# Idle tags for gelu rows, earlier block-sum stores, a later normalisation and slots by readiness in a two-layer attention and gMLP kernel

## The chip, the cores and the metric

The kernel runs on one core of one Trainium2 chip. A core has five engines with a queue of instructions each: TensorE (PE, matrix products), VectorE (DVE), ScalarE (ACT), GpSimd (POOL) and SyncE (SP, which here issues nearly all transfers). They run side by side and wait for one another through semaphores. The metric is the device time of one launch in microseconds (us), as the median of several runs; less is better. Beside the times there is one profiled execution, whose trace gives the start, the length and the releaser of every instruction.

## The reference: what is computed

One sequence of 2048 tokens with 512 features passes four blocks, each with a layer norm ahead of it and a residual: linear attention, gated MLP, linear attention, gated MLP, with the same weights in both layers. All is float32.

```python
# attention: 32 heads of 16
pq, pk = phi(q), phi(k)                    # phi(t) = (t + 1 if t > 0 else exp(t)) + 1e-6
kv  = einsum("bhsd,bhse->bhde", pk, v);  z = pk.sum over tokens
o   = (pq @ kv) / (pq . z + 1e-6);         x = x + o @ wo
# gated MLP: w_in is 512 x 1792, two halves of 896
z   = gelu(layernorm(x) @ w_in)
z1  = z[..., :896];  z2 = layernorm(z[..., 896:])
g   = w_sp @ z2 + b_sp[:, None]            # w_sp is 2048 x 2048, over the tokens
x   = x + (z1 * g) @ w_out
```

## The kernel before

**Arithmetic.** Each matrix operand is split into a high and a low part (`high`, L133, on ScalarE; `low`, L136, on VectorE), and each product is three matmuls: high by high, high by low, low by high (`mm3`, L147 to L149). TensorE is therefore fed by pairs of tiles, and a product starts when the high part is there.

**Order.** The order of the instructions of each engine is the order in which the program issues them; no scheduler moves anything. A token tile is 128 rows, so there are 16.

**Storage.** Fast memory is cut into slots: 23 `pages` of 128x512, six `quads` four times as large, four `bigs`, and eight banks of accumulators. `Slots.get` takes the free slot with the smallest count and `Slots.put` gives one back with a lag, so that a slot still being stored is not taken at once; it counts takings and not time. Beside them stand 16 tags (`ztag`), one for each token tile: tag i holds first the attention query of tile i, then (as `z_turn`) the normalised tile on its way through a transposition, block sums in between, and at last the z2 tile itself. `Views` (L63) cuts two spare quads into eight page-size views for the piece of work in P1 that follows; it hands them out in the order in which they came back, and turns to the pages only when no view is left.

**Stages of a layer.** P1 goes over the tiles: layer norm, projections of key and query, phi, and the accumulation of the key products. Beside that it prepares sums of blocks of w_sp, a row at a time, for later use (`Inner.staged`): load, add on VectorE, split, store to scratch as `n`; its slots come from `Views`. A short transition forms the weights of the attention output. P2 (`P2.run`, steps s = 1 to 18) works on four tiles at once, at different depths: `b_high`/`b_low` split the attention operand of tile s; `c` multiplies tile s - 1 and `c3` stores the new x, normalises it into `z_turn` and sends it through scratch memory (`yt`: a store and a load in another layout, then a 32x32 transpose on VectorE, L328); `d_high`/`d_low` split tile s - 2; `e` multiplies tile s - 3 by the second half of w_in, `e2` applies gelu, `e3` takes statistics, and `e4` normalises a tile that passed `e3`, for the last tile after the loop. In each step two rows of the first half of w_in are multiplied as well (`f`): the gelu row goes into a page (L924), is stored to scratch as `z1` (L927) and read by the gates much later. In layer one, step s ends with `sums.tick(s, TOKEN_TICKS)`: it stores the block sums of w_sp that were added one tick ago (`Sums.store`, L1194), loads the blocks for the next ones (L1187) into z tags that are free and else into pages, and adds them on GpSimd (`Sums.add`, L1201).

After P2 comes `tail` (L1017 on): the last f row (`last_f`), and products P3, P6, P7, P4 and P5 of a block scheme for the remaining f rows, with copies of results on ScalarE (`copied`, L997) and additions on VectorE (L1031). P4 is the spatial product by w_sp in a scheme with fewer products; each unit g of it needs a split weight (L1445 on ScalarE, L1454 on VectorE) and a split operand (L1424 to L1426, L1450, L1458), and TensorE runs 18 or 24 matmuls a unit (L1607 to L1609). In layer one `sums.tick(g, MIX_TICKS)` prepares the rest of the block sums beside it. Gates and the output product end the layer.

SyncE issues its transfers in program order. A transfer that has to wait for its data holds up all that are behind it.

Of the kernel before, what the change touches and what calls it, by code (L numbers as in the profile page):

```python
# [15 lines left out]
P = 128  # L16
# [3 lines left out]
NT = S // P  # L20
# [5 lines left out]
PHI_EPS = 1e-6  # L26
DEFER = 6
STORE, POOL = 6, 3
TOKEN_TICKS = {5: (5, 6), 6: (7,), 8: (8, 9), 9: (10,), 11: (11, 12), 12: (13,), 13: (14,), 14: (15,)}
MIX_TICKS = (1, 4, 7, 8, 10, 12, 14, 16, 20, 21, 23, 24, 26, 27, 29, 30, 32, 34, 35, 37, 38, 39, 40, 41)  # L30
MIX_UNITS = (11, 15, 18, 20, 25, 31, 36, 40), (1, 3, 5, 7, 9, 11, 13, 15)
MAKE_AT = 5, 8, 11
ROW_UNITS = range(1, 9)
# [4 lines left out]
class Slots:  # L38


    def __init__(self, pool, prefix, n):
        self.pool, self.prefix = pool, prefix
        self.free_list = [(0, i) for i in range(n)]
        self.held = {}
        self.count = 0

    def get(self, shape, dtype=F32):
        assert self.free_list, f"no {self.prefix} slot"
        first = min(self.free_list, key=lambda e: e[0])
        self.free_list.remove(first)  # L50
        n = first[1]
        self.count += 1
        t = self.pool.tile(shape, dtype, tag=f"{self.prefix}{n}", bufs=1, name=f"{self.prefix}{n}_{self.count}")
        self.held[id(t)] = (n, t)
        return t

    def put(self, *tiles, lag=0):
        for t in tiles:
            n, _ = self.held.pop(id(t))
            self.free_list.append((self.count + lag, n))  # L60


class Views:  # L63


    def __init__(self, pages, *tiles):
        self.pages = pages
        self.free_list = deque(t[:, n // 2, n % 2] for n in range(4) for t in tiles)
        self.held = {}

    def get(self, shape, dtype=F32):
        if not self.free_list:
            return self.pages.get(shape, dtype)
        t = self.free_list.popleft()
        self.held[id(t)] = t
        return t

    def put(self, t, lag=0):
        if id(t) not in self.held:
            self.pages.put(t, lag=lag)  # L80
            return
        self.free_list.append(self.held.pop(id(t)))

    def close(self):
        assert not self.held
# [3 lines left out]
def mixer_kernel(ctx: ExitStack, tc: tile.TileContext, x_in, wqkv, wo_d, win1_d, win2_d, wsp_d, bsp_d, wout_d,  # L89
                 ident_d, mask_d, out_d):  # L90
    nc = tc.nc
# [7 lines left out]
    pages = Slots(main, "pg", 23)  # L99
# [4 lines left out]
    PAGE = [P, 512]  # L104
    ztile = {}

    def ztag(i, shape, kind, dtype=F32):
        t = main.tile(shape, dtype, tag=f"z{i}", bufs=1, name=f"z{i}_{kind}")
        ztile[i] = t
        return t  # L110

    ident = consts.tile([P, P], F32, name="ident")
    ones_f = pages.get(PAGE)
    nc.vector.memset(ones_f, 1.0)

    mhalf = consts.tile([P, 1], F32, name="mhalf")
    nc.vector.memset(mhalf, -0.5)
# [17 lines left out]
    def low(l, src, h):  # L135
        nc.vector.tensor_sub(l, src, h.bitcast(F32))  # L136
# [155 lines left out]
    class Turn:  # L292
# [22 lines left out]
        def load(self, i):  # L315
            if i in self.d:
                self.raw[i] = load(self.d.pop(i).rearrange("(p m) f -> p (m f)", m=4))
# [15 lines left out]
    class P1:  # L333
# [158 lines left out]
        def start(self):  # L492

            nc.gpsimd.affine_select(ident, ones_f[:, 0:P], pattern=[[1, P]], compare_op=OP.is_equal, fill=0.0, base=0,
                                    channel_multiplier=-1)
            self.loadx(0)
            self.loadx(1)
            for w in (self.wk, self.wq):
                for _ in range(4):
                    w.fetch()  # L500
            self.loadx(2)
            self.loadx(3)
            m = pages.get(PAGE, F32R)
            nc.vector.tensor_copy(m, ones_f)
            b = banks.get(PAGE)

            def idle(n):
                for _ in range(n):
                    nc.tensor.matmul(b, m[:, 0:P], m, start=True, stop=True)

            idle(9)
            lows = deque()

            def wk_low():
                l, src, h, r = lows.popleft()
                low(l, src, h)
                pages.put(r)

            self.ln_a(0)
            self.ln_a(1)  # L520
            self.ln_b(0)
            self.wk.piece(lows=lows)
            wk_low()
            self.T_high(0)
            idle(2)
            banks.put(b)
            pages.put(m, ones_f)
            self.T_low(0)
            for _ in range(2):
                self.wk.piece(lows=lows)  # L530
                wk_low()
            self.ln_b(1)
            self.wk.piece(lows=lows)
            wk_low()
            b = self.kb[0] = banks.get(PAGE)
            h, l = self.xT[0]
            w = self.wk

            def mm(x, y, c, **kw):
                nc.tensor.matmul(b, x[:, c, :], y[:, c, :], start=kw.get("start", False), stop=kw.get("stop", False))  # L540

            mm(h, w.h, 0, start=True)
            mm(h, w.l, 0)
            mm(h, w.h, 1)
            mm(l, w.h, 0)
            mm(l, w.h, 1)
            mm(h, w.l, 1)
            mm(h, w.h, 2)
            mm(l, w.h, 2)
            self.T(1)  # L550
            mm(h, w.l, 2)
            mm(h, w.h, 3)
            mm(l, w.h, 3)
            mm(h, w.l, 3, stop=True)
            self.ln_a(2)
            for _ in range(4):
                self.wq.piece()
            self.ln_b(2)
# [210 lines left out]
    class P2:  # L769
# [139 lines left out]
                H1, H2 = self.p4.H1, self.p4.H2  # L909
                nc.vector.tensor_sub(z[:, H2], z[:, H1], z[:, H2])  # L910

        def f(self):
            if not self.fq:
                return False
            n, f = self.fq.popleft()
            h, l = self.xT[n]
            w = self.win1
            b = banks.get(PAGE)
            for c in range(4):
                mm3(b, (w.h[:, f, c, :], w.l[:, f, c, :]), (h[:, c, :], l[:, c, :]), c == 0, c == 3)  # L920
            if f == NF - 1 and n < 2:
                quads.put(*self.xT.pop(n))
            t = pages.get(PAGE)
            nc.scalar.activation(t, b, AF.Gelu_apprx_tanh)  # L924
            banks.put(b)
            z1s[self.L, n, f] = dram.tile(PAGE, F32, name=f"z1_{self.L}_{n}_{f}")
            nc.sync.dma_start(z1s[self.L, n, f], t)  # L927
            pages.put(t, lag=STORE)
            return True

        def gelu_out(self, n, f, t, src=None):
# [85 lines left out]
        def tail(self, p4):  # L1017
            self.last_f(3)
            U2, U3 = [], []
            for g in range(3):  # L1020
                y = banks.get(PAGE)
                self.product(y, "P3", g, start=True, stop=True)
                U2.append(self.copied(y))
                banks.put(y)
            quads.put(*self.xT.pop(3))
            self.fetch_sum(1)
            p4.fetch(0)
            p4.fetch(1)
            for g in range(3):
                self.product(self.X[g], "P6", g)  # L1030
                nc.vector.tensor_add(U2[g], U2[g], self.X[g])  # L1031
            quads.put(self.Tp[2])
            for g in range(3):
                self.product(self.X[g], "P7", g)
                U3.append(self.copied(self.X[g]))
            quads.put(self.Tp[3])
            p4.prepare(0, 0)
            p4.fetch(2)
            for g in range(3):
                self.product(self.X[g], "P4", g, stop=True)  # L1040
                self.gelu_out(2, g + 3, pages.get(PAGE), self.X[g])
                banks.put(self.X[g])
            quads.put(self.Tp[4])
            self.win1.free()
            p4.prepare(1, 1)
            p4.fetch(3)
            for g in range(3):
                y = banks.get(PAGE)
                self.product(y, "P5", g, start=True, stop=True)
                for n, f, t in ((3, g + 3, U3[g]), (3, g, U2[g])):  # L1050
                    nc.vector.tensor_add(t, t, y)
                    p4.outs.append((n, f, t))
                banks.put(y)
            quads.put(self.Tp[1])
            p4.prepare(None, 2)
# [20 lines left out]
        def run(self, sums):  # L1076
# [3 lines left out]
            for s in range(1, NT + 3):  # L1080
# [58 lines left out]
                if s > 6:  # L1139
                    self.e4(s - 4)  # L1140
                self.xturn.load(s - 1)
                if s >= 3:
                    self.e(s - 3)
                    self.e2(s - 3)
                if s >= 6:
                    self.e3(s - 3)
                self.f()
                self.f()
                self.side(s)
                if self.L == 0:  # L1150
                    make.step(s)
# [7 lines left out]
                w1.fetch()  # L1159
                if self.L == 0:  # L1160
                    sums.tick(s, TOKEN_TICKS)
            self.e4(NT - 1)
            self.win2.free()


# [185 lines left out]
    class P4:  # L1351
# [395 lines left out]
        def run(self, nxt):  # L1747
# [13 lines left out]
            for g in range(n):  # L1761
# [8 lines left out]
                if self.nest_late:  # L1770
                    self.sums.tick(g, MIX_TICKS)
                    if g == 34:
# [88 lines left out]
    sums = Sums()  # L1861
# [45 lines left out]
```

## Time and profile before

| | us |
|---|---|
| median of 3 runs | 1373.98 |
| lowest and highest | 1371.97, 1375.28 |
| profiled execution | 1371.57 |
| its span, first to last instruction | 1369.8 |
| TensorE busy | 1358.0 |
| VectorE busy | 1024.6 |
| ScalarE busy | 636.7 |
| GpSimd busy | 467.5 |

Times in the rows below count from the start of the span. A row of the timeline gives the start, the length, the engine, the line, the operation and, in square brackets, how long the engine stood idle before it and what released it (`<-`). The first column of a slice table is the stretch, then follow its length, the busy time of each engine, the granted clock of TensorE, the share of the transfer engines in use and the rate in GB/s. Tiles are named by their slots: pg a page, qd a quad, bg a big one, z_q, z_z, z_sum and z_turn the uses of a tag. Where a transfer row has `x2`, two issues stand together. In layer one the residual additions of P2 (L843) stand from 146.7 to 311.7 us, and the first matmul of the spatial product (L1608) starts at 354.2.

### The profile page before, as it was taken

What the parts mean: (1) busy time and instruction counts of PE and PEld (TensorE: products, weight loads), DVE (VectorE), ACT (ScalarE), POOL (GpSimd) and SP (SyncE); (2) the same over time, 40 slices, a digit from 0 to 9 for tenths busy, and PEclk for the clock granted to TensorE, in tenths of its full rate; (3) what the DMA queues carried; (4) which work ended last, traced back from release to release, by engine and by line L of the source; (5) the groups of instructions that cost most, each with busy time, mean ns of one, the idle gap of its engine ahead of it and who ended that gap; (6) DMA issues with size and microseconds to landing.
All of it is one profiled execution on the core that took longest, in us unless ns stands there. A gap on an engine that the chain in (4) does not pass through costs nothing.

```text
span 1369.8 us, 18327 instructions
## 1 busy us (share of the span) xinstructions
PE 1358.0 (99%) x6087; PEld 1132.0 (83%) x6087; DVE 1024.6 (75%) x1581; ACT 636.7 (46%) x1021; POOL 467.5 (34%) x551
## 2 busy tenths in 40 slices
PE   9999999999999999999999999999999999999998
PEld 7788888878888888888888888888888888888887
DVE  7886888767855888986678768887767798978642
ACT  6675544435442443442456655444455534533310
POOL 2334385453143337426421133633230011412340
PEclk9999999999999999999999999999999999999999
DMA  5673378886788988895776533666568798569652
GB/s 187 203 233 95 123 251 266 281 270 196 241 284 284 304 273 276 274 391 180 221 253 202 194 101 114 210 205 206 189 197 277 226 336 322 187 200 314 216 186 89
DMA packets 184496, 310.18 MB, mean 226 GB/s; under 512 B 15696, under 2 KB 67920, under 8 KB 180304
## 3 DMA queue, kind: packets, MB, share of 16 engines
q1 hardware_dynamic: 172736, 262.73, 58.6%
q0 software_dynamic: 8064, 39.85, 8.3%
q10 hardware_dynamic: 3600, 6.42, 1.3%
q8 instruction: 48, 0.79, 0.2%
q14 instruction: 48, 0.39, 0.1%
HBM read 211.68 MB, written 97.26 MB: 226 GB/s over the span
## 4 chain that ended last, share of the span: by engine, by line
PE 71%; DVE 3%; DMA 2%; issue 1%; ACT 1%; POOL 0%; SPq 0%; DVEq 0%; ACTq 0%; POOLq 0%
PE bank L149 11%; PE bank L147 10%; PE bank L148 10%; PE bank L1608 9%; PE bank L1607 9%; PE bank L1609 9%; PE bank L1540 4%; PE bank L1541 4%; PE bank L1538 4%; PE bank L989 1%; PE bank L991 1%; PE bank L990 1%; DMA yt<-z_turn 1%; DMA pg<-yt 0%; DVE st L262 0%
## 5 line engine op out<-in xcount | busy, mean ns | idle before, releaser
L1608 PE MATMUL bank<-qd,pg 128*128 128x512 f32 x544 | 211.7, 389 | 0.5 <-DVE qd L1454 0.5
L1609 PE MATMUL bank<-qd,pg 128*128 128x512 f32 x544 | 211.6, 389 | 0.0
L1607 PE MATMUL bank<-qd,pg 128*128 128x512 f32 x544 | 211.6, 389 | 0.0
L1454 DVE TENSOR_TENSOR qd<-qd,qd 128x1024 fp32r<-128x1024 f32 x104 | 142.3, 1368 | 65.5 <-ACT qd L1445 65.0
L1445 ACT ACTIVATE qd<-qd 128x1024 fp32r<-128x1024 f32 x104 | 110.0, 1058 | 121.9 <-DVE qd L1454 44.1
L149 PE MATMUL bank<-qd,pg 128*128 128x512 f32 x380 | 149.0, 392 | 0.5 <-DVE pg L136 0.4
L133 ACT ACTIVATE pg<-pg 128x512 fp32r<-128x512 f32 (+1 forms) x146 | 89.2, 620 | 123.1 <-DVE pg L328 38.2
L266 POOL TENSOR_SCALAR rs<-mv 128x1 f32<-128x1 f32 x95 | 42.6, 448 | 273.4 <-DVE mv L264 269.3
L1629 POOL TENSOR_TENSOR bg<-bg,pg 128x512 f32<-128x512 f32 x56 | 91.7, 1648 | 107.0 <-DMA pg<-z 98.1
L136 DVE TENSOR_TENSOR pg<-pg,pg 128x512 fp32r<-128x512 f32 (+1 forms) x143 | 108.4, 759 | 20.4 <-ACT pg L133 15.8
L1608 PEld LDWEIGHTS bank<-qd,pg 128*128 128x128 f32 x544 | 102.1, 188 | 22.1 <-DVE qd L1454 0.9
L1607 PEld LDWEIGHTS bank<-qd,pg 128*128 128x128 f32 x544 | 102.1, 188 | 21.2
L1609 PEld LDWEIGHTS bank<-qd,pg 128*128 128x128 f32 x544 | 102.1, 188 | 21.2
L1201 POOL TENSOR_TENSOR pg<-pg,pg 128x512 f32<-128x512 f32 x45 | 67.3, 1495 | 137.6 <-DMA pg<-in_wsp_dram 116.8
L147 PE MATMUL bank<-qd,pg 128*128 128x512 f32 x284 | 110.9, 391 | 0.5 <-ACT pg L133 0.5
L148 PE MATMUL bank<-qd,pg 128*128 128x512 f32 x284 | 110.6, 390 | 0.0
L147 PE MATMUL bank<-bg,qd 128*128 128x448 f32 x256 | 95.1, 371 | 2.8 <-ACT qd L133 2.7
L149 PE MATMUL bank<-bg,qd 128*128 128x448 f32 x256 | 94.5, 369 | 0.2
L148 PE MATMUL bank<-bg,qd 128*128 128x448 f32 x256 | 94.2, 368 | 0.0
L328 DVE STREAM_TRANSPOSE pg<-pg 128x512 f32<-128x512 f32 x79 | 86.0, 1088 | 6.0 <-DMA pg<-yt 2.9
L1540 PE MATMUL bank<-qd,pg 128*128 128x512 f32 x224 | 87.4, 390 | 0.3 <-DVE qd L1454 0.3
L1538 PE MATMUL bank<-qd,pg 128*128 128x512 f32 x224 | 87.2, 389 | 0.0
(218 smaller groups left out, 3193.3 us busy)
## 6 DMA issues: line engine op xcount, KB each, us to landing
qd<-s SPq DMA_DIRECT2D x64, 512.0 KB, 4.0
qd<-n POOLq DMA_DIRECT2D x32, 1024.0 KB, 7.5
pg<-in_wsp_dram SPq DMA_DIRECT2D x84, 256.0 KB, 4.7
qd<-in_wsp_dram SPq DMA_DIRECT2D x40, 512.0 KB, 4.2
pg<-z SPq DMA_DIRECT2D x56, 256.0 KB, 3.9
n<-pg SPq DMA_DIRECT2D x54, 256.0 KB, 4.5
s<-pg SPq DMA_DIRECT2D x53, 256.0 KB, 4.4
x<-pg SPq DMA_DIRECT2D x48, 256.0 KB, 2.7
```

The costliest lines, as they stand in the source:

```text
L136: nc.vector.tensor_sub(l, src, h.bitcast(F32))
L147: nc.tensor.matmul(out, ah, bh, start=start, stop=False)
L148: nc.tensor.matmul(out, ah, bl, start=False, stop=False)
L149: nc.tensor.matmul(out, al, bh, start=False, stop=stop)
L1445: nc.scalar.activation(wh, r, AF.Copy)
L1454: nc.vector.tensor_sub(wl, r, wh.bitcast(F32))
L1538: m(out[i], h[:, o, f], w[:, o, 0], start=first and name in ("P1", "P2", "P5"), stop=False, skip_group_check=True)
L1540: m(out[i], h[:, o, f], w[:, o, 1], start=False, stop=False, skip_group_check=True)
L1607: m(out, h[:, o], w[:, 0, j, :], start=start, stop=False, skip_group_check=True)
L1608: m(out, h[:, o], w[:, 1, j, :], start=False, stop=False, skip_group_check=True)
L1609: m(out, l[:, o], w[:, 0, j, :], start=False, stop=stop, skip_group_check=True)
L1629: nc.gpsimd.tensor_tensor(u, u, z1, op=OP.mult)
```

## The change

Six edits, all in the order or the place of work that is done before and after alike.

1. `Views` keeps with each view the count at which it is due back. `get` hands out a view only if it is due, or if no page is due either; else it takes a page.
2. `f` takes an optional tag. In both layers the first gelu row of step s goes into tag s + 2 where that is below 16, and in layer one the second goes into the tag that `SPARE_TAGS` names for the step; else a page is used as before.
3. `TOKEN_TICKS` gives each fetch of block sums one tag, the number of its step, where before some got two and the fetches at 6, 9, 12, 13 and 14 a tag one higher. The other two blocks go to pages.
4. In layer one `sums.store()` is called in the middle of each step of P2, right behind the load of the turned tile, and no longer at its end.
5. `e4` of the last tile moves from the end of the P2 loop into `tail`, behind the three P3 products and their copies.
6. The first entry of `MIX_TICKS` is 2 instead of 1. And `ones_f`, a page of ones for the start, is set in two instructions, the first 128 columns and then the rest.

```diff
-TOKEN_TICKS = {5: (5, 6), 6: (7,), 8: (8, 9), 9: (10,), 11: (11, 12), 12: (13,), 13: (14,), 14: (15,)}
-MIX_TICKS = (1, 4, 7, 8, ...
+TOKEN_TICKS = {at: (at,) for at in (5, 6, 8, 9, 11, 12, 13, 14)}
+SPARE_TAGS = {6: 7, 8: 7, 9: 10, 11: 10, 14: 15, 16: 15}
+MIX_TICKS = (2, 4, 7, 8, ...
...
 class Views:
-        self.free_list = deque(t[:, n // 2, n % 2] for n in range(4) for t in tiles)
+        self.free_list = deque((0, t[:, n // 2, n % 2]) for n in range(4) for t in tiles)
...
     def get(self, shape, dtype=F32):
-        if not self.free_list:
+        now = self.pages.count
+        if not self.free_list or (self.free_list[0][0] > now and any(r <= now for r, _ in self.pages.free_list)):
             return self.pages.get(shape, dtype)
-        t = self.free_list.popleft()
+        _, t = self.free_list.popleft()
...
     def put(self, t, lag=0):
...
-        self.free_list.append(self.held.pop(id(t)))
+        self.free_list.append((self.pages.count + lag, self.held.pop(id(t))))
...
-    nc.vector.memset(ones_f, 1.0)
+    nc.vector.memset(ones_f[:, 0:P], 1.0)
...
+            nc.vector.memset(ones_f[:, P:], 1.0)
             nc.vector.tensor_copy(m, ones_f)
...
-        def f(self):
+        def f(self, tag=None):
...
-            t = pages.get(PAGE)
+            t = pages.get(PAGE) if tag is None or tag >= NT else ztag(tag, PAGE, "out")
...
             nc.sync.dma_start(z1s[self.L, n, f], t)
-            pages.put(t, lag=STORE)
+            if id(t) in pages.held:
+                pages.put(t, lag=STORE)
...
         def tail(self, p4):
...
                 banks.put(y)
+            self.e4(NT - 1)
             quads.put(*self.xT.pop(3))
...
         def run(self, sums):
...
                 self.xturn.load(s - 1)
+                if self.L == 0:
+                    sums.store()
                 if s >= 3:
                     self.e(s - 3)
...
-                self.f()
-                self.f()
+                self.f(s + 2)
+                self.f(SPARE_TAGS.get(s) if self.L == 0 else None)
...
-            self.e4(NT - 1)
             self.win2.free()
```

More of the change, by code (lines that the diff above doesn't have):

```diff
@@ L28 @@
 STORE, POOL = 6, 3
-TOKEN_TICKS = {5: (5, 6), 6: (7,), 8: (8, 9), 9: (10,), 11: (11, 12), 12: (13,), 13: (14,), 14: (15,)}
-MIX_TICKS = (1, 4, 7, 8, 10, 12, 14, 16, 20, 21, 23, 24, 26, 27, 29, 30, 32, 34, 35, 37, 38, 39, 40, 41)
+TOKEN_TICKS = {at: (at,) for at in (5, 6, 8, 9, 11, 12, 13, 14)}
+SPARE_TAGS = {6: 7, 8: 7, 9: 10, 11: 10, 14: 15, 16: 15}
+MIX_TICKS = (2, 4, 7, 8, 10, 12, 14, 16, 20, 21, 23, 24, 26, 27, 29, 30, 32, 34, 35, 37, 38, 39, 40, 41)
 MIX_UNITS = (11, 15, 18, 20, 25, 31, 36, 40), (1, 3, 5, 7, 9, 11, 13, 15)
```

## The prediction

> **What bounds the kernel now.** I read the page first, then the waits of TensorE, then the instructions around each wait in the timeline, engine by engine.
>
> ```profile
> span 1369.8 us, 18327 instructions
> PE 1358.0 (99%) x6087; PEld 1132.0 (83%) x6087; DVE 1024.6 (75%) x1581; ACT 636.7 (46%) x1021; POOL 467.5 (34%) x551
> ```
>
> TensorE is busy for 1358.0 of 1369.8 us. The change removes no matmul, so it can only win back idle time, 11.8 us in all, and what the clock loses around it. The waits of TensorE (total, times, longest):
>
> ```profile
> PE bank L147 <- ACT qd L133: 2.7, 2, 2.0
> PE bank L989 <- DVE pg L1031: 1.0, 1, 1.0
> ```
>
> The timeline of TensorE at four of its waits, all in layer one, and the slice table for the longest:
>
> ```profile
> 63.75 0.39 PE L149 MATMUL bank<-pg,pg 128*128 128x512 f32 x1
> 64.67 0.50 PE L147 MATMUL bank<-qd,pg 128*128 128x512 f32 x1 [0.53 <-ACT pg L133]
> ...
> 65.74 0.39 PE L147 MATMUL bank<-qd,pg 128*128 128x512 f32 x1
> ...
> 284.70 0.47 PE L147 MATMUL bank<-bg,qd 128*128 128x448 f32 x1 [2.01 <-ACT qd L133]
> ...
> 340.03 0.39 PE L990 MATMUL bank<-qd,pg 128*128 128x512 f32 x1
> 340.26 0.39 PE L991 MATMUL bank<-qd,pg 128*128 128x512 f32 x1
> 341.64 0.50 PE L989 MATMUL bank<-qd,pg 128*128 128x512 f32 x1 [0.99 <-DVE pg L1031]
> ...
> 364.90 0.39 PE L1607 MATMUL bank<-qd,pg 128*128 128x512 f32 x1
> 365.80 0.50 PE L1608 MATMUL bank<-qd,pg 128*128 128x512 f32 x1 [0.51 <-DVE qd L1454]
> ...
> 371.41 0.39 PE L1608 MATMUL bank<-qd,pg 128*128 128x512 f32 x1
> ```
>
> ```profile
> 280.00:300.00 20.00, 17.81 (x74) 15.04 (x75) 13.28 (x22) 9.19 (x15) 9.04 (x14) 0.91 0.91 302
> ```
>
> Undisturbed matmuls of 512 columns start 0.23 us apart (340.03 to 340.26). A wait costs its start-to-start time less 0.23. From 63.75 to 65.74 four intervals took 1.99 instead of 0.92: 1.07 lost. From 340.26 to 341.64: 1.38 less 0.23 is 1.15. From 364.90 to 365.80: 0.90 less 0.23 is 0.67. The wait before 284.70 cost 2.01, and the clock granted in its slice is 0.91 of full speed, some 0.09 x 20 = 1.8 more: 3.8 together.
>
> **Part by part.** *Spare quads by readiness (Views).* The timelines of ScalarE and VectorE ahead of 64.67:
>
> ```profile
> 60.28 0.63 ACT L133 ACTIVATE qd<-qd 128x512 fp32r<-128x512 f32 x1 [2.09 <-DMA n<-qd]
> ...
> 63.99 0.63 ACT L133 ACTIVATE pg<-pg 128x512 fp32r<-128x512 f32 x1 [0.69 <-PE bank L148]
> ```
>
> ```profile
> 62.10 0.69 DVE L417 SCALAR_TENSOR_TENSOR z_q<-bank,z_q 128x512 f32<-128x512 f32 x1 [2.22 <-ACT z_q L416]
> 62.81 1.09 DVE L328 STREAM_TRANSPOSE pg<-pg 128x512 f32<-128x512 f32 x1
> ```
>
> At 60.28 the block-sum piece writes a view of a spare quad whose last store (DMA n<-qd) has not landed; ScalarE stands for 2.09. The query projection's exponentials are queued behind it, VectorE's L417 waits 2.22 for them, the transpose L328 follows at 62.81, and the operand that TensorE wants is written at 63.99 to 64.62, 0.05 before 64.67. The named releaser of 63.99 (a matmul) is long done; the transpose is what came last. The change gives this piece a page that is already free, so the chain moves up by about 2 us, more than the 1.07 that TensorE lost. Gain between 0 (if what follows catches up) and 1.07; I take 1.0, because nothing in that row set but ScalarE's wait was late.
>
> *Gelu rows in idle tags, sums stored mid-step.* What VectorE waits for in layer one's second half, and SyncE's issues there:
>
> ```profile
> 264.59 0.88 DVE L136 TENSOR_TENSOR pg<-pg,pg 128x512 fp32r<-128x512 f32 x1 [1.81 <-DMA z<-pg]
> ...
> 279.38 0.69 DVE L136 TENSOR_TENSOR pg<-pg,pg 128x512 fp32r<-128x512 f32 x1 [1.59 <-DMA z<-pg]
> ```
>
> ```profile
> 276.05 0.86 SPq L927 DMA_DIRECT2D z<-pg  x2
> ...
> 278.20 1.62 SPq L1194 DMA_DIRECT2D s<-z_sum  x2
> ```
>
> Both L136 write the low half of the attention operand (b_low) into a page whose gelu row is still being stored. With gelu rows in z tags the first wait goes. The second stays: the slots are reused in count order, and in the new order the page that b_low of step 13 draws is that of a block sum, whose store now is issued in the very place of the gelu row's, right behind the yt load (276.05 instead of 278.20). So it lands when the gelu row landed, and L136 starts at about 279.4 again. No DMA is added or dropped; the three sum stores move ahead of two gelu-row stores and two win_sums stores, each of which goes to scratch that nobody reads for many steps. What decides the wait at 284.70 is further on:
>
> ```profile
> 284.69 0.57 SPq L313 DMA_DIRECT2D yt<-z_turn  x1
> 290.18 0.32 SPq L129 DMA_DIRECT2D pg<-yt  x1
> ```
>
> The chain of waits runs through the turn of each tile: store to scratch (yt), landing 5.5 us later, load, transpose, split, the matmuls of e. SyncE issues in order and its count per step is unchanged. So I put this part at 0 on the path, between -3.8 (the wait at 284.70 goes with its clock loss) and the worst price of the next paragraph.
>
> *One tag per fetch, tags in use sooner.* A tag now carries a sum, its store, and the next turned tile closer together: ScalarE's z_turn (L277) waits for the sum's store to land. The landing times of all sum stores between 250 and 330 us (least, median, most), the z_turn of step 15, and SyncE's place right behind the yt load, which the sum stores take:
>
> ```profile
> DMA to landing us min/median/max: 3.3/3.7/4.2
> ```
>
> ```profile
> 306.89 0.80 ACT L277 ACTIVATE z_turn<-pg,nb,rs 128x512 f32<-128x512 f32 x1
> ```
>
> ```profile
> 302.07 0.94 SPq L228 DMA_DIRECT2D win_sums<-pg  x2
> ```
>
> The z_sum goes second, at about 302.55, and with 3.7 lands at 306.25, 0.6 ahead of the z_turn. Steps 14 and 16 are built alike. I take 0; with the longest landing, 4.2, and no margin in one of them, 0.5 at worst. Behind z_turn stand the yt store and, one step on, e.
>
> *Last tile normalised in the tail (e4).* POOL, ScalarE and VectorE before 341.64:
>
> ```profile
> 337.40 1.32 POOL L271 TENSOR_SCALAR nb<-mv,rs 128x1 f32<-128x1 f32 x1
> ```
>
> ```profile
> 338.76 1.14 ACT L277 ACTIVATE z_z<-z_z,nb,rs 128x896 f32<-128x896 f32 x1 [2.17 <-POOL nb L271]
> 339.80 0.58 ACT L924 ACTIVATE pg<-bank 128x512 f32<-128x512 f32 x1
> ```
>
> ```profile
> 340.89 1.29 DVE L1031 TENSOR_TENSOR pg<-pg,bank 128x512 f32<-128x512 f32 x2 [1.62 <-ACT pg L997]
> ```
>
> The normalisation of tile 15 holds ScalarE for 2.17 us until POOL's nb; the gelu row of last_f (L924), the U2 copies (L997), and VectorE's L1031, for which TensorE waits, are queued behind it. Moved behind the three P3 products, it lets L924 start 338.76 - 2.17 = 336.6, over 3 us sooner, and the copies with it. VectorE had been idle for 1.62 before 340.89, so L1031 can start at 339.3 and end its first half (1.29 / 2) near 339.9, ahead of 340.49, where TensorE would want it. All 1.15 is gained, at least 0.99 less the 0.23 of a matmul if the copies come late. It also lets SyncE's gelu-row store go sooner, and so the first two spatial fetches behind it. Cost: the normalisation of tile 15 itself ends some 1 to 2 us later; the spatial product reads that tile only in its later operands. I count 0 for it, and the copies cover it.
>
> *First block sum of the spatial product one unit later (MIX_TICKS).* POOL's three additions, and VectorE beside and after them:
>
> ```profile
> 359.44 4.55 POOL L1201 TENSOR_TENSOR pg<-pg,pg 128x512 f32<-128x512 f32 x3 [19.07 <-PE bank L1608]
> ```
>
> ```profile
> 361.20 1.64 DVE L1424 TENSOR_TENSOR z_z<-z_z,z_z 128x384 f32<-128x384 f32 x1
> 362.87 1.53 DVE L1425 TENSOR_TENSOR pg<-z_z,z_z 128x384 f32<-128x384 f32 x1
> ...
> 364.53 1.21 DVE L1454 TENSOR_TENSOR qd<-qd,qd 128x1024 fp32r<-128x1024 f32 x1
> ...
> 366.26 0.55 DVE L1424 TENSOR_TENSOR z_z<-z_z,z_z 128x384 f32<-128x384 f32 x1
> ...
> 367.52 1.22 DVE L1454 TENSOR_TENSOR qd<-qd,qd 128x1024 fp32r<-128x1024 f32 x1
> ```
>
> Two subtractions of 128x384 took 1.64 and 1.53 beside the additions, and 0.55 without: 2.07 in excess, which made L1454 end at 365.74, 0.06 before 365.80. Without it L1454 ends near 363.7, with over 1 us to spare, and the 0.67 is gained. One unit later the same 2.07 falls on the operand whose split ended at 368.74 with that excess still in it and that TensorE wants from 371.41: 2.67 to spare, 2.0 after the gain. Gain 0.67, at worst 0.67 less 2.07.
> [...]
>
> *The memset in two pieces.*
>
> ```profile
> 0.97 0.48 DVE L114 MEMSET pg<- 128x512 f32 x1 [0.97 <-PEq L1896]
> ```
>
> The same 512 columns are set, in one more instruction; 0, at most 0.48 either way. Layer two gets the tags and the readiness rule as well; its waits are none of the ones above, and I count 0.
>
> The sum: 1.0 + 1.15 + 0.67 = 2.8 us, rounded up to 2.9 for the slower first matmul behind each wait (0.50 against 0.39 at 341.64 and 365.80). The profiled execution took 1371.57 us (its span is 1369.8), 2.4 below the median of the runs, 1373.98. So the profiled execution would become 1368.7 and the median about **1371.1**.
>
> **The rivals.** *One: the wait at 284.70 goes too.* If the sum's store lands sooner than the gelu row's did, or TensorE's wait is cut enough that the clock holds, up to 3.8 more is won, 1367.3. For it: one of the two store waits is gone. Against: the other is replaced, the yt chain ends last, and the row of the waits has a second wait of 0.7 (2.7 less 2.0) on the same chain that would absorb part of it; I would expect about half, 1369.
> [...]
>
> *Two: half of it does not show.* The 1.0 at 64.67 is given back, because what follows in that stage is paced by loads and not by TensorE; 1.9 is left, 1372.1, no measurable change. If the page drawn at step 13 is freed later than reckoned (its store kept at 278.20, landing at 281.9, 2.6 after 279.38), the loss of 2.6 eats almost all: 1373.7.
>
> *Three: slower, by tags.* Under the load of this stage other stores of the same size take longer to land (x rows, the same stretch, least, median, most):
>
> ```profile
> DMA to landing us min/median/max: 3.8/5.2/6.6
> ```
>
> If the sum stores, now among them, take 6.6 instead of 3.7, the z_turn of step 15 starts 2.3 late (6.6 less the 4.3 between 302.55 and 306.89), and with it yt, transpose and e; if steps 14 and 16 do the same, three of them add up to 6.9, less 2.9: +4.0, 1378.0. It decides from a landing of 4.3 us on; at 5.2 it is three times 0.9, and 1373.8.
>
> **How the numbers follow.** A change of 0.2%, 2.7 us, is about what a measurement of this kernel can tell from none; from 1373.98 that is 1371.2 to 1376.7. The forecast has 0.50; its own range, 1369.8 to 1372.3, has a little more than half below 1371.2, so 0.28 faster and 0.22 same. Rival one has 0.16, all faster; two 0.14, all same; three 0.20, of which 0.03 for its mild form (5.2), same, and 0.17 slower. Faster 0.44, same 0.39, slower 0.17. The range, 1366.8 to 1377.0, takes in all of one and two and the lower half of three; it leaves out some 0.1 above and what the scatter of the runs adds.
>
> **What would show it.** In the changed profile: no wait of ScalarE on n<-qd near 60 and none of TensorE at 64.7; no wait on L1031 near 338 and on L1454 near 362; the long additions of POOL one unit later. The wait of e near 282 should still be there with a granted clock near 0.9. Wrong it would be if that wait is gone, or if ScalarE's z_turn waits on a sum store.

## The result and the profile after

| | before | after |
|---|---|---|
| median, 12 runs each (us) | 1373.88 | 1369.03 |
| lowest and highest | 1371.61, 1376.39 | 1367.73, 1371.06 |
| profiled execution | 1371.57 | 1370.24 |

The ratio is 0.9965 with a 95% interval of 0.9956 to 0.9974, so 4.9 us were won (3.6 to 6.0), where 2.9 were forecast. The two profiled executions differ by 1.3 only: that of before lies 2.3 below its median, that of after 1.2 above its own. One pair of profiles shows where the time goes, but not how much of it goes there in the usual execution; the experiments have to tell that.

The page of the changed kernel, its first lines, and the waits of TensorE (total, times, longest; the changed kernel's L149 is L147 of before, L135 is L133, L512 is L509):

```profile
span 1368.5 us, 18313 instructions
...
PE 1356.4 (99%) x6087; PEld 1131.3 (83%) x6087; DVE 1026.7 (75%) x1582; ACT 637.6 (47%) x1021; POOL 468.0 (34%) x551
```

```profile
PE bank L149 <- ACT qd L135: 5.2, 4, 1.5
PE bank L512 <- DVE pg L507: 2.0, 1, 2.0
PE bank L151 <- DVE pg L138: 0.5, 2, 0.3
```

The waits on L1031 (tail) and L1454 (spatial product) are gone, and so is that at 64.7. In their place stands a longer sum for one line: the product e waits four times for its split operand (5.2 us, where the line had 2.7 in two waits). The slice table of the changed kernel (stretch, length, busy time of TensorE, its weight loads, VectorE, ScalarE and GpSimd, clock, transfers' share, GB/s):

```profile
60.00:80.00 20.00, 20.00 (x90) 16.54 (x89) 18.21 (x31) 16.44 (x29) 6.79 (x11) 1.00 0.82 259
...
280.00:300.00 20.00, 17.08 (x77) 13.79 (x76) 11.46 (x19) 9.08 (x15) 9.93 (x16) 1.00 0.87 278
300.00:320.00 20.00, 17.52 (x78) 13.74 (x77) 15.41 (x28) 8.42 (x13) 7.05 (x12) 1.00 0.67 229
...
340.00:360.00 20.00, 20.00 (x90) 16.57 (x89) 13.31 (x24) 8.23 (x13) 0.70 (x2) 1.00 0.63 207
360.00:380.00 20.00, 20.00 (x90) 16.57 (x89) 18.75 (x26) 12.10 (x18) 5.88 (x4) 1.00 0.78 263
```

TensorE is full in the three slices (60 to 80, 340 to 360, 360 to 380) where the prediction found a wait that goes, and short by 2.9 and 2.5 us in the two slices of layer one's second half. The timeline of TensorE there:

```profile
283.17 0.47 PE L149 MATMUL bank<-bg,qd 128*128 128x448 f32 x1 [1.32 <-ACT qd L135]
294.32 0.47 PE L149 MATMUL bank<-bg,qd 128*128 128x448 f32 x1 [1.50 <-ACT qd L135]
306.39 0.47 PE L149 MATMUL bank<-bg,qd 128*128 128x448 f32 x1 [0.89 <-ACT qd L135]
316.04 0.47 PE L149 MATMUL bank<-bg,qd 128*128 128x448 f32 x1 [1.48 <-ACT qd L135]
```

Before, the four were 2.01 (with a drop of the clock), none worth naming, 0.66 and 0.12. Two of the waits behind them are ones that the prediction named: on VectorE (b_low of step 13), as a wait that stays, and on ScalarE (z_turn of step 16), at 0.5 at worst:

```profile
277.84 0.69 DVE L138 TENSOR_TENSOR pg<-pg,pg 128x512 fp32r<-128x512 f32 x1 [1.79 <-DMA s<-pg]
```

```profile
316.34 0.81 ACT L279 ACTIVATE z_turn<-pg,nb,rs 128x512 f32<-128x512 f32 x1 [0.35 <-DMA s<-z_sum]
```

The gelu row's store (1.59, z<-pg) has been replaced by the sum's (1.79, s<-pg) as the releaser of b_low. The trip of the turned tile through scratch, on SyncE's queue, is longer than before:

```profile
283.12 1.03 SPq L315 DMA_DIRECT2D yt<-z_turn  x1
289.40 0.32 SPq L131 DMA_DIRECT2D pg<-yt  x1
...
295.43 0.61 SPq L315 DMA_DIRECT2D yt<-z_turn  x1
301.72 0.32 SPq L131 DMA_DIRECT2D pg<-yt  x1
```

Each load waits 6.3 us for the store ahead of it to land; in the profile of before the two took 5.5 and 5.4. In the second profiles (below) it is 5.9 and 5.6 for the changed kernel, 4.9 and 5.0 for the kernel before.

### The profile page after: what moved, and what is told of

It is laid out like the page before. It is cut to its first block, busy times and chain, and to the rows that moved or that the text cites. A ratio compares the mean times of both kernels' runs of the same rounds, so it can differ in the third digit from the quotient of the medians.

```text
span 1368.5 us, 18313 instructions
## 1 busy us (share of the span) xinstructions
PE 1356.4 (99%) x6087; PEld 1131.3 (83%) x6087; DVE 1026.7 (75%) x1582; ACT 637.6 (47%) x1021; POOL 468.0 (34%) x551
## 3 DMA queue, kind: packets, MB, share of 16 engines
q1 hardware_dynamic: 172736, 262.73, 58.9%
## 4 chain that ended last, share of the span: by engine, by line
PE 76%; DVE 3%; DMA 3%; ACT 1%; issue 1%; POOL 1%; SPq 0%; DVEq 0%; ACTq 0%; POOLq 0%
PE bank L151 11%; PE bank L149 11%; PE bank L150 11%; PE bank L1613 9%; PE bank L1614 9%; PE bank L1615 9%; PE bank L1546 4%; PE bank L1544 4%; PE bank L1547 4%; DMA yt<-z_turn 1%; PE bank L994 1%; PE bank L993 1%; PE bank L995 1%; DMA pg<-yt 1%; DVE pg L138 1%
## 5 line engine op out<-in xcount | busy, mean ns | idle before, releaser
L1460 DVE TENSOR_TENSOR qd<-qd,qd 128x1024 fp32r<-128x1024 f32 x104 | 143.4, 1380 | 67.8 <-ACT qd L1451 67.4
L135 ACT ACTIVATE pg<-pg 128x512 fp32r<-128x512 f32 (+1 forms) x146 | 89.3, 620 | 123.8 <-DVE pg L330 47.2
L268 POOL TENSOR_SCALAR rs<-mv 128x1 f32<-128x1 f32 x95 | 42.2, 444 | 266.6 <-DVE mv L266 258.0
L1207 POOL TENSOR_TENSOR pg<-pg,pg 128x512 f32<-128x512 f32 x48 | 70.8, 1475 | 138.0 <-DMA pg<-in_wsp_dram 113.9
L149 PE MATMUL bank<-qd,pg 128*128 128x512 f32 x284 | 110.9, 390 | 0.2 <-ACT pg L135 0.2
L149 PE MATMUL bank<-bg,qd 128*128 128x448 f32 x256 | 94.6, 370 | 5.2 <-ACT qd L135 5.2
```

The source lines that it names most:

```text
L149: nc.tensor.matmul(out, ah, bh, start=start, stop=False)
L1460: nc.vector.tensor_sub(wl, r, wh.bitcast(F32))
```

## The experiments

Each was compared with the kernel before on its own chip; "won" is the ratio's distance from 1, times 1374.

| run | what | median (us) | ratio, interval | won (us) |
|---|---|---|---|---|
| e1_rest | all but tags and stores | 1369.24 | 0.9957, 0.9944 to 0.9971 | 5.9 |
| e2_p2 | tags and stores alone | 1375.07 | 0.9995, 0.9986 to 1.0004 | 0.7 |
| e5_views | readiness alone | 1371.09 | 0.9970, 0.9958 to 0.9981 | 4.1 |
| e6_tail | normalisation in the tail alone | 1373.51 | 0.9993, 0.9984 to 1.0001 | 1.0 |
| e7_mix | first block sum later, alone | 1374.30 | 0.9995, 0.9986 to 1.0004 | 0.7 |
| e8_early_fetch | the changed kernel, sums' transfers ahead of the yt load | 1367.40 | 0.9948, 0.9936 to 0.9961 | 7.1 |
| e9_mid_tick | and GpSimd's additions with them | 1364.48 | 0.9922, 0.9909 to 0.9935 | 10.7 |
| e10_mid_tick_x | and the x store behind the yt store | 1366.29 | 0.9934, 0.9922 to 0.9946 | 9.1 |

**The two halves of the change, and second profiles.** My theory on record was: three waits go, 2.9 us, and the second half of layer one stays as it is (A). Against it stood that the second half is worth as much again (B), and that arriving there earlier changes what its transfers meet (C).

e1_rest:

```diff
 # e1_rest, against after.py (f itself as before, too)
-TOKEN_TICKS = {at: (at,) for at in (5, 6, 8, 9, 11, 12, 13, 14)}
-SPARE_TAGS = {6: 7, 8: 7, 9: 10, 11: 10, 14: 15, 16: 15}
+TOKEN_TICKS = {5: (5, 6), 6: (7,), 8: (8, 9), 9: (10,), 11: (11, 12), 12: (13,), 13: (14,), 14: (15,)}
...
-                if self.L == 0:
-                    sums.store()
...
-                self.f(s + 2)
-                self.f(SPARE_TAGS.get(s) if self.L == 0 else None)
+                self.f()
+                self.f()
```

> Before plus the readiness of the spare quads, the last tile's normalisation in the tail, the first block sum one unit later and the memset in two; nothing of the gelu rows, tags and sum stores. Theory A (on record: these three waits go, the attention and gMLP half of layer one stays as it is): 2.9 us faster than before, ratio 0.9979, and in the profile no wait of TensorE at 64.7, 341.6 and 365.8, the wait of 2 us near 284 as before. Theory B (the stores and tags are worth as much again in the median run, and the profile of before was a good one): the same 2.9 here. Theory C (the earlier arrival at the second half is what helps, because it changes what its transfers meet): 4 to 5 us faster here, ratio near 0.9967.

e2_p2 is the kernel before with just these edits of the change and none of the others.

> Before plus the gelu rows and block sums in tags and the sum stores mid-step; nothing else of the change. Theory A: within 0.5 us of before, ratio 1.000; in the profile VectorE waits for a sum's store instead of a gelu row's at b_low of step 13. Theory B: 2 us faster, ratio 0.9985. Theory C: no change, or slightly slower, up to 1 us, as the four waits of the profile of the changed kernel (1.32, 1.50, 0.89, 1.48) against those of before (2.01 with its clock loss, 0.66, 0.12) would have it.

> The kernel before, unchanged, for a second profile of it. If the waits of TensorE between 280 and 320 us vary from execution to execution (theory B), they come to more here than the 2.8 us of idle and 1.9 us of lost clock in the first profile, by 1 to 3 us, and the time is nearer to 1374; if they do not (theory A), they are the same within 0.5 us.

> The changed kernel, unchanged, for a second profile. Its first had 5.2 us of waits for the split operand of the second half (1.32, 1.50, 0.89, 1.48) and 1370.24 us, 1.2 over its median. Theory B: those waits come to 1 us or more less here, with a time near 1369. Theory A: the same within 0.5 us.

e1_rest won 5.9 us and its median, 1369.24, is that of the whole change; e2_p2 won 0.7 with an interval that holds 1. So the second half's edits are not worth the 2 us that B gave them, and A is right about the second half and wrong about the size of the rest. C's number came, but not where C looked for it: the profile of e1_rest has the same waits in the second half as that of before, 1.98, 0.67 and 0.35 against 2.01, 0.66 and 0.12. So C falls too. In the profile of e2_p2 b_low of step 13 waits for a sum's store, as A expected, but for 3.16 us, and the waits of e there sum to 4.6.

The second profiles (1372.81 before, 1368.56 after) are split. B expected of the changed kernel 1 us or more less of these waits, and they sum to 3.9 instead of 5.2; it expected of the kernel before 1 to 3 us more than the first profile lost there, and the waits sum to 3.5 with the clock at 1.00, less than the 2.8 us and the lost clock of the first. So the second half does vary from execution to execution. The hint came from another stage: in the second profile of before TensorE also loses time at 56, 96 to 99 and 118, in the stage of the spare quads, where the first had none.

**The three other edits one by one.**

```diff
 # e5_views, before.py with
-        if not self.free_list:
+        now = self.pages.count
+        if not self.free_list or (self.free_list[0][0] > now and any(r <= now for r, _ in self.pages.free_list)):
             return self.pages.get(shape, dtype)
...
 # e6_tail, before.py with
+            self.e4(NT - 1)
             quads.put(*self.xT.pop(3))
...
-            self.e4(NT - 1)
             self.win2.free()
...
 # e7_mix, before.py with
-MIX_TICKS = (1, 4, 7, 8, ...
+MIX_TICKS = (2, 4, 7, 8, ...
```

> Before plus the readiness of the spare quads alone. Step of the prediction: 1.0 us faster, the one wait at 64.7. Rival: the late ScalarE of that stage costs TensorE more in a usual execution than in the first profile of before; the second profile of it lost 2.6 us between 30 and 120 us of the span (at 56, 64, 96, 99 and 118) and the kernel with the second half's edits alone 4.0, against 0.7 with readiness. Then 2 to 3 us faster, ratio 0.9978 to 0.9985, and 0.7 us or so lost there in its profile.

> Before plus the last tile's normalisation in the tail alone. Step of the prediction: 1.15 us faster, ratio 0.9992, no wait of TensorE for VectorE's L1031 in the tail. Rival: the earlier first fetches of the spatial product are worth something too: up to 2 us, ratio 0.9985.

> Before plus the first block sum of the spatial product one unit later, alone. Step of the prediction: 0.7 to 0.8 us faster, ratio 0.9995, no wait for L1454 near 366; the additions lengthen VectorE's operations one unit later without a wait of TensorE. [...] The three alone should add up to what the kernel with all three won, 4 to 6 us, if they do not act on one another; if the sum stays below 3.5, they do.

They won 4.1, 1.0 and 0.7 us: 5.8 in sum, and 5.9 together, so nothing shows that they act on one another, though each figure is uncertain by about 1 us. The tail and the block sum came out near the predicted 1.15 and 0.67, but the interval of each reaches to 1; the profiles, which settle these two, follow below. Readiness was sized too small: 1.0 against 4.1, with an interval from 2.6 to 5.8. The memset in two pieces was tried only together with the others; in the first 20 us TensorE is neither ahead nor behind with it, beyond the 0.5 us by which the profiles without it differ among themselves.

Where its time comes from is seen in the profile of e6_tail, which still has the old `Views`. The slice of that stage, first of e6_tail and then of e5_views:

```profile
30.00:125.00 95.00, 92.95 (x398) 73.31 (x397) 75.24 (x120) 65.61 (x111) 32.38 (x46) 1.00 0.67 197
```

```profile
30.00:125.00 95.00, 94.96 (x418) 78.00 (x417) 77.16 (x123) 67.44 (x114) 33.21 (x47) 1.00 0.67 203
```

In the same 95 us TensorE starts 20 matmuls fewer in e6_tail, some 4.5 us of work at 0.23 each. Without readiness the five profiles had 415 (the first one of before), 410, 408, 402 and 398 there, with it all seven had 417 to 419. The prediction worked from the best of the five. In e6_tail the waits of TensorE, of ScalarE between 60 and 120 us, and VectorE's transpose at the end of the stage read:

```profile
PE bank L147 <- ACT pg L133: 1.1, 1, 1.1
PE bank L147 <- ACT z_h L133: 0.8, 1, 0.8
```

```profile
ACT z_h L133 <- DVE pg L328: 6.2, 6, 3.8
ACT bg L133 <- DMA pg<-in_win_dram: 4.3, 5, 1.8
ACT pg L431 <- DVE pg L417: 3.9, 4, 1.1
ACT qd L133 <- DMA n<-qd: 2.2, 1, 2.2
```

```profile
118.01 1.09 DVE L328 STREAM_TRANSPOSE pg<-pg 128x512 f32<-128x512 f32 x1 [2.44 <-DMA pg<-xt]
```

and in e5_views, ScalarE in the same stretch:

```profile
ACT pg L416 <- PE bank L150: 6.8, 8, 2.3
```

With readiness ScalarE waits for TensorE: it is ahead. Without, it waits for loads and transposes, and not once for TensorE in e6_tail: two waits for a view's store to land (n<-qd, 2.02 ending at 51.12 and 2.22 ending at 60.93) have put it behind, and the normalised tiles that it sends through scratch (xt) leave late. These two waits stand in all five profiles without readiness (1.6 to 2.2 us each) and in none of the seven with it. The last load of such a tile is issued at 113.15 in e6_tail and at 108.70 in e5_views. TensorE then meets one late operand (the first profile of before) or several (at 65.3, 92.9, 96 and 118.6 in e6_tail). That the landings of the moment decide which is likely, but not shown.

**From one matmul to the same matmul.** TensorE runs its 6087 matmuls in the same order in all twelve profiles, so the time between two of them can be compared across kernels. It measures a stage without the scatter of the rest of the execution. In us, the stretches named by the first profile of before:

| stretch of TensorE | first profile of before | others without the edit | with the edit |
|---|---|---|---|
| spare quads, 30.08 to 125.17 | 95.1 | 96.0 to 98.8 (four) | 94.0 to 94.4 (seven) |
| end of layer one's P2, 270.18 to 330.04 | 59.9 | 58.9 to 60.6 (five) | 61.1, 59.7 (the changed kernel), 61.9 (e2_p2) |
| tail, 340.03 to 350.16 | 10.13 | 9.72 to 10.03 (four) | 8.84 (seven) |
| first block sum, 364.22 to 380.02 | 15.81 | 15.99 to 16.57 (four) | 14.96 (seven) |

So the tail gives 0.9 to 1.3 us and the block sum 0.8 to 1.6 in every profile; both gains are shown, although the medians alone could not tell them from nothing. Readiness gives 0.7 to 4.8, by the means of the two groups 2.6.

**What ends last in the second half.** The changed kernel still loses the most there, so I tested the reading of its SyncE queue: the store of the turned tile lands late because the loads of the next block sums lie ahead of it, and SyncE stands idle in front of the yt load, for up to 5.6 us, where it could issue them.

```diff
 # e8_early_fetch, after.py with
-                self.xturn.load(s - 1)
                 if self.L == 0:
                     sums.store()
+                    if s + 1 in TOKEN_TICKS:
+                        sums.fetch(TOKEN_TICKS[s + 1])
+                self.xturn.load(s - 1)
...
-            if i + 1 in at:
+            if i + 1 in at and not isinstance(at, dict):
                 self.fetch(at[i + 1] if isinstance(at, dict) else ())
```

> The changed kernel with the loads of the next block sums and the sum stores issued ahead of the load of the turned tile, while SyncE waits for that tile's store to land, instead of behind it. If the landing of the turned tile's store (5.5 to 6.3 us) is long because those loads lie ahead of it in the transfer queues, it falls to 3 to 4 us in steps 13 to 15, the four waits for the split operand between 280 and 320 us (5.2 and 3.9 us in the two profiles) fall below 2 us, and the time is 2 to 4 us below the changed kernel's, near 1366. If the landing is long for another reason, the time stays within 0.7 us of 1369.

SyncE's queue and TensorE in its profile:

```profile
293.53 0.37 SPq L315 DMA_DIRECT2D yt<-z_turn  x1
...
295.86 0.37 SPq L131 DMA_DIRECT2D pg<-yt  x1
```

```profile
281.82 0.47 PE L149 MATMUL bank<-bg,qd 128*128 128x448 f32 x1 [0.28 <-ACT qd L135]
291.94 0.47 PE L149 MATMUL bank<-bg,qd 128*128 128x448 f32 x1 [0.56 <-ACT qd L135]
303.32 0.47 PE L149 MATMUL bank<-bg,qd 128*128 128x448 f32 x1 [0.47 <-ACT qd L135]
313.04 0.47 PE L149 MATMUL bank<-bg,qd 128*128 128x448 f32 x1 [1.53 <-ACT qd L135]
```

From the yt store to the load behind it are 2.3 us instead of 6.3 in step 14, below the 3 to 4 that I expected: what lay ahead in the queue did make it late. But the waits fall from 5.2 to 2.8, not below 2, because the last one stays, and the median falls by 1.6, short of the expected 2 to 4; the intervals of the two kernels, each against its own before, still overlap. GpSimd in that profile shows what is late next:

```profile
298.17 1.29 POOL L1209 TENSOR_TENSOR pg<-z_sum,pg 128x512 f32<-128x512 f32 x1
299.54 1.62 POOL L1209 TENSOR_TENSOR z_sum<-z_sum,pg 128x512 f32<-128x512 f32 x1
301.25 1.30 POOL L1209 TENSOR_TENSOR pg<-pg,pg 128x512 f32<-128x512 f32 x1
302.63 0.22 POOL L268 TENSOR_SCALAR rs<-mv 128x1 f32<-128x1 f32 x1
```

The statistics of the tile to be turned (L268) run straight behind three additions.

```diff
 # e9_mid_tick, after.py with
-                self.xturn.load(s - 1)
                 if self.L == 0:
-                    sums.store()
+                    sums.tick(s, TOKEN_TICKS)
+                self.xturn.load(s - 1)
...
                 w1.fetch()
-                if self.L == 0:
-                    sums.tick(s, TOKEN_TICKS)
...
 # e10_mid_tick_x, that and in c3
-            nc.sync.dma_start(xs[2 * self.L + 1, i], x)
             turned = self.xturn.turned(i)
...
+            self.xturn.store(i, y)
+            nc.sync.dma_start(xs[2 * self.L + 1, i], x)
             pages.put(x, lag=STORE)
-            self.xturn.store(i, y)
```

> As the kernel with the early fetches, and the additions on GpSimd moved with them, from the end of the step to its middle, behind the statistics of the tile that is about to be turned. If GpSimd's additions are what is late next (in the early-fetch profile three of them, 298.2 to 302.6, stand ahead of the statistics at 302.63 that the turned tile waits for, which were wanted from 301.6), the last of the four waits (1.53) falls to about 0.5 and the others are at most what they were: 1.0 to 1.5 us below the early-fetch kernel, ratio to the kernel before near 0.994. If the transfers still set the end there, no change against it, ratio 0.995.

> The same, and the store of the new x (256 KB) issued behind the store of the turned tile instead of ahead of it, in both layers. If transfers ahead in the queues still lengthen the turned tile's landing, it falls by up to 0.8 us a step in layer one's second half: another 0.5 to 1 us. If not, no change within 0.5 us.

In e9_mid_tick the waits of e for ScalarE are gone; what is left is three waits for the low part on VectorE, 1.9 us in all. Two stand in the same stretch. The third, ahead of them, is new, and part of what the edit costs:

```profile
232.63 0.47 PE L151 MATMUL bank<-bg,qd 128*128 128x448 f32 x1 [0.69 <-DVE qd L138]
...
282.70 0.47 PE L151 MATMUL bank<-bg,qd 128*128 128x448 f32 x1 [0.32 <-DVE qd L138]
293.07 0.47 PE L151 MATMUL bank<-bg,qd 128*128 128x448 f32 x1 [0.88 <-DVE qd L138]
```

It won 10.7 us on the kernel before, 2.9 below the early fetch by the medians, more than the 1.0 to 1.5 expected: the two waits at 303.3 and 313.0 are gone altogether, and not only the last of them cut to 0.5. The stretch from 270.18 to 330.04 in the table above takes 58.3 us in e8_early_fetch and 55.2 here. It is the fastest version tried, with 1364.48 against 1369.03, and its interval is clear of that of the changed kernel. The x store behind the yt store did not help; its median is 1.8 above, with intervals that overlap, while its profile, the fastest of its runs, has the same waits (0.60 and 0.87 in place of 0.32 and 0.88). Whether it is slower, and why, was not followed up.

## Why the prediction was right or wrong

**The range and the sign** held: 1369.03 lies between 1366.8 and 1377.0, faster by 4.9. The range is 10 us wide, so that says little. The likeliest time was 2.1 too high.

**The three gains together.** In the first pair of profiles, from matmul to matmul, readiness gives 0.74 us (1.0 taken), the tail 1.29 (1.15) and the block sum 0.85 (0.67): 2.88, where the sum had 2.8, rounded up to 2.9. As an account of this one execution of the kernel before the working is right, and that is more than the time alone would show. The second half took 1.2 more in the same pair, which is why the two profiled executions differ by 1.3 only.

**Readiness of the spare quads, 1.0 taken, 4.1 measured** (2.6 to 5.8): the term of the sum that was mis-sized. The prediction bounded the gain by the 1.07 that TensorE lost at 64.7, "because nothing in that row set but ScalarE's wait was late". The mechanism was right, but the upper bound came from one execution, and that one was the best of five. In the other four TensorE takes 0.9 to 3.7 us longer for the same stretch, which the first profile did not show at all. The profiles' mean gain of 2.6 is at the lower end of the measured interval; what makes the rest of the 4.1, if it is real, was not found in a row. What spoke for more could be seen. ScalarE's waits for a bank of TensorE between 60 and 120 us, first in the profile of before and then in that of the changed kernel:

```profile
ACT pg L415 <- PE bank L149: 1.0, 1, 1.0
```

```profile
ACT pg L417 <- PE bank L151: 6.6, 7, 2.3
```

In the first profile ScalarE was ahead of TensorE once, for 1.0 us (a second row of 0.7 that names a matmul is the wait at 63.99, which ended with the transpose). So it had next to nothing in hand, and any landing a little later had to reach TensorE.

**Gelu rows in tags, sums stored mid-step, 0 taken, 0.7 measured with 1 in the interval.** With the other edits in place the whole change won 4.9 and e1_rest, which lacks these, 5.9, so 0 is as good a figure as any that the runs can tell. One part of the reason held: the first b_low wait goes, the second is taken over by the sum's store in the gelu row's place (1.59 and 1.79). The other did not: the wait at 284.7 neither stayed as it was nor stayed alone. It is 1.32 us with the clock at 1.00, where the prediction expected a clock near 0.9, and three other waits grew. That the two nearly cancel was not foreseen, and is luck. The prediction took the count of SyncE's issues for all that sets this chain; what lies ahead of the yt store in the queue decides as well, as e8_early_fetch shows.

**z_turn on its tag, 0 taken, 0.5 at worst:** 0.35 in step 16 and nothing in steps 14 and 15. A wait of z_turn on a sum store was one of the two signs by which the prediction would call itself wrong. It came, within the price given for it: the margin of 0.6 read from step 15 was not there in step 16, although it was taken to be built alike. Rival three, the same mechanism at 6.6 us a landing, did not come: the sum stores landed in 3.2 to 4.1 us.

**The tail, 1.15, and the block sum, 0.67:** measured 1.0 and 0.7, and in the first pair of profiles 1.29 and 0.85. The rows answer the working of the tail. In the tail ScalarE runs the copies first, L1001, and the normalisation behind them:

```profile
337.65 1.56 ACT L1001 ACTIVATE pg<-bank 128x512 f32<-128x512 f32 x3
339.09 1.14 ACT L279 ACTIVATE z_z<-z_z,nb,rs 128x896 f32<-128x896 f32 x1
```

and VectorE's first addition starts at 339.53, where 339.3 was reckoned. The additions of the first block sum have moved behind 365, and the subtractions of 128x384 there are lengthened to the very figures that they had before, without a wait of TensorE:

```profile
364.96 4.74 POOL L1207 TENSOR_TENSOR pg<-pg,pg 128x512 f32<-128x512 f32 x3 [24.27 <-DMA pg<-in_wsp_dram]
```

```profile
365.21 1.78 DVE L1464 TENSOR_TENSOR pg<-pg,pg 128x512 fp32r<-128x512 f32 x1
366.92 1.64 DVE L1430 TENSOR_TENSOR z_z<-z_z,z_z 128x384 f32<-128x384 f32 x1
368.59 1.53 DVE L1431 TENSOR_TENSOR pg<-z_z,z_z 128x384 f32<-128x384 f32 x1
...
370.25 1.21 DVE L1460 TENSOR_TENSOR qd<-qd,qd 128x1024 fp32r<-128x1024 f32 x1
```

```profile
375.53 0.39 PE L1614 MATMUL bank<-qd,pg 128*128 128x512 f32 x1
```

But the working had the new place wrong. TensorE runs 24 matmuls a unit here, so by that count the low parts of the split weights are wanted at 364.65, 370.09 and 375.53, and VectorE's splits (L1460) end at 362.29, 365.29 and 371.46. The additions fall on the third, not on the second as the prediction had it, and there 4.1 us were to spare, with the excess in it, and not 2.0. It also left out the third lengthened operation (L1464, 1.78 against 0.68): the excess is 3.2 us in all and not 2.07. The gain is as forecast because the slack was larger too. Beside the 4.74 us of additions these 3.2 are all the excess that the rows show; an excess of the whole 4.74 would still have left 2.5 to spare at the third.

**Rival one** priced the wait at 284.7 with 1.8 for the clock. In the profile of after, the clock is at 1.00 throughout, and that gain was eaten by the three grown waits. It does not belong to the change either: of the six profiles without the tags only three show the drop. **The median** was made from the profile's difference on the assumption that both stand alike to their medians; they stood 2.3 below and 1.2 above. The profiled execution, put at 1368.7, took 1370.24.

## What to carry to other kernels

A wait off the critical engine can be worth more than what the critical engine lost behind it in one profile (here 4.1 us against 1.07): look whether the engine that waits is ever ahead of the critical one in that stage, and if it is not, take a second profile before you bound the gain. Where the order of the critical engine's instructions does not change, compare the time between the same two of them: that measured the tail and the block sum here, which the medians could not. Where an in-order transfer queue stands before a load that waits for its own store, the transfers that come next belong in that gap, ahead of the load, and behind the store that all wait for: here the load went out 2.3 us behind that store in step 14, instead of 6.3, and the median fell by 1.6. And when one chain is shortened, ask what else is queued ahead of its next link on each engine: here, once the transfers were out of the way, GpSimd's additions were worth another 2.9 us by the medians.

## What the runs showed of the hardware

A wait of TensorE of about 2 us was sometimes followed by a lower granted clock and sometimes not. The waits of 2.01, 1.99 and 1.98 (before, e6_tail, e1_rest) were followed by a granted clock of 0.91 in the slice, those of 2.02 and 1.93 (e2_p2, the second profile of before) by 1.00, and so were those of 1.71, 1.67 and 1.64 (e5_views, e7_mix, the second profile of after). In before, matmuls of 448 columns start 0.20 us apart after the wait, and from some 1.9 us behind its end nine of them start 0.37 apart, which is 1.5 us lost. So the length alone does not decide it, and what else does was not shown. The slice of e2_p2, with the longest of them:

```profile
280.00:300.00 20.00, 15.95 (x68) 11.87 (x66) 12.03 (x18) 6.04 (x10) 8.38 (x13) 1.00 0.87 273
```
